# Attention and feed-forward mix: the plain input loads first on SyncE's queue, the first transposing transfers in halves

## The chip, the cores and the metric

The kernel runs on one core of one Trainium2 chip. A core has five engines, each with its own stream of instructions: TensorE (PE) multiplies matrices, VectorE (DVE) and ScalarE (ACT) work on whole tiles, GpSimd (POOL) does smaller tile work, and SyncE (SP) issues most DMA transfers. SyncE and ScalarE each have a DMA queue; in the profile SyncE's packets are counted under q1 and ScalarE's under q10. Both queues feed the same 16 DMA engines. The metric is the device time of one execution in microseconds (us).

## The reference

The inputs are x with 2,048 tokens of 512 columns in bf16, and weights. Attention has 32 heads of 16 columns, the feed-forward part an inner width of 1,792. A gate per token mixes the two:

```python
g = sigmoid((x * gate_w).sum(-1, keepdims=True))
a = attention(x, wqkv, 32 heads) @ wo       # softmax over all 2,048 tokens
b = (silu(x @ w_gate) * (x @ w_up)) @ w_down
return g * a + (1 - g) * b
```

## The kernel before

Nearly every product needs x with its columns on the partitions. That is the tile xT, `[128, 4, 2048]`: four blocks of 128 columns (dc 0 to 3), each with all 2,048 tokens. It is filled in two ways:

- By transposing DMA transfers from SyncE's queue (`queue`, line 292 on): first dc 0 and 1 for the tokens 0 to 1,023, then dc 0 to 3 for the tokens 1,024 to 2,047, one transfer of 1,024 tokens by 128 columns each, six in all.
- For dc 2 and 3 of the first 1,024 tokens by TensorE: two plain loads on ScalarE's queue (line 290) put those columns, rows as they are, into `x_rows`, a part of the tile wd_t that is needed only later. TensorE turns them, 128 by 128, by products with the identity (`turn`), and ScalarE (dc 3) and VectorE (dc 2) copy the results to xT.

Behind the row loads ScalarE's queue carries the 64 columns of K weights and the 64 columns of Q weights for the first group of heads (line 297). ScalarE spreads each into a padded tile (`pad(1)` for K, `pad(0)` for Q; the tile is called mt in the profile), and after `pad(1)` issues the load of the first 64 columns of V weights (tile rb, line 361). SyncE's queue carries, behind the transposes, the other V weights (rb), then the other K and Q weights (wqk), then the small gate column.

The opening is written out by hand. TensorE runs 12 products on zeros (`keep_warm(12)`, which write the same bank), then the 16 turns in four groups of four: dc 3 of tokens 0 to 511, dc 2 of the same, dc 3 of tokens 512 to 1,023, dc 2 of those. ScalarE's order is: the queue's issues, the table load, one small activation, `pad(1)`, the V load's issue, the copies of turn groups one and three, `pad(0)`. Then TensorE makes K for the first 1,024 tokens with eight products, and Q for the first 512 with eight half-width ones:

```python
arrived = (3, 0, 2, 1)
for tb, dc in ((tb, dc) for tb in range(2) for dc in arrived):
    mm(kp0[:, tb * QBW:(tb + 1) * QBW], lhsT=wpad[1][:, dc, :], rhs=xT[:, dc, tb * QBW:(tb + 1) * QBW],
       start=(dc == arrived[0]), stop=(dc == arrived[-1]))
```

A bound of the scores is taken from K's largest values and Q, and the first scores go to ScalarE as exponentials (tile e_all). From there a planner in the kernel's text orders the work: it keeps a model of each engine's time, and at each step writes out score products, products with V, projections or feed-forward pieces. All of that is fixed when the kernel is built; on the chip each engine runs its list in order and waits on semaphores. K of tokens 1,024 to 2,047 (`k0_pieces`) is the first side work, right behind the first scores, and needs the last four transposing transfers.

Every DMA of SyncE's and ScalarE's queues takes the next of eight semaphores in turn; a transfer waits, before it is issued, until the earlier transfer on its semaphore has landed.

Of the kernel before, what the change touches and what calls it, by code (L numbers as in the profile page):

```python
# [82 lines left out]
def kernel(  # L83
# [12 lines left out]
    nc = tc.nc  # L96
    P = 128
    x = A_x.flatten_outer_dims()
    S, D = x.shape
# [5 lines left out]
    DC = D // P  # L105
    FC = F // P
    KT = S // P
    QBW = 512
    QB = S // QBW
    TQ = QBW // P  # L110
# [171 lines left out]
    queue = Ordered(nc.sync)  # L282


    xT = big.tile([P, DC, S], BF16, name="xT")
    wd_t = big.tile([P, FC, D], BF16, name="wd_t")
    HALF = DC // 2
    x_rows = wd_t[:, 0:4, :].rearrange("p f d -> p (f d)").rearrange("p (i d) -> p i d", d=HALF * P)
    for t0 in range(2):
        nc.scalar.dma_start(out=x_rows[:, TQ * t0:TQ * t0 + TQ, :], in_=x[t0 * QBW:(t0 + 1) * QBW, HALF * P:D].rearrange("(i p) d -> p i d", p=P))  # L290
    for t0 in (0, 2 * QBW):
        for dc in range(DC if t0 else HALF):
            queue.dma_start_transpose(out=xT[:, dc, t0:t0 + 2 * QBW], in_=x[t0:t0 + 2 * QBW, dc * P:(dc + 1) * P])
    wqk = big.tile([P, DC, 2 * D], BF16, name="wqk")
    for c0 in (D, 0):

        nc.scalar.dma_start(out=wqk[:, :, c0:c0 + 64],
                            in_=A_wqkv[:, c0:c0 + 64].rearrange("(dc p) c -> p dc c", p=P))
# [5 lines left out]
    for c0 in (D, 0):  # L304
        queue.dma_start(out=wqk[:, :, c0 + 64:c0 + D],
                          in_=A_wqkv[:, c0 + 64:c0 + D].rearrange("(dc p) c -> p dc c", p=P))
# [373 lines left out]
    def q_pieces(qb, b):  # L680
        def landed(p):
            me = plan.chain
            later(0.6, lambda: end(p, me), key=("q", b))

        def rows(t, r):
            for hh in range(8):
                gg, j = hh // 4, hh % 4
                if (b, gg) != (0, 0):
                    queue.dma_start(out=get_q(qb, 2 * b + gg)[32 * j + r:32 * j + r + DH, j % 2, :],
                                      in_=t[DH * hh:DH * (hh + 1), :])  # L690

        def end(p, me):
            qst = work.tile([P, QBW], BF16, tag="qst", name="qst")
            vec.tensor_copy(out=qst[:, :], in_=p[:, :])
            m_free(p, plan.dve)
            rows(qst, 0)

            aq = work.tile([P, QBW], BF16, tag="aq", name="aq")

            def mag():  # L700
                vec.tensor_scalar(out=aq[:, :].bitcast(U16), in0=qst[:, :].bitcast(U16), scalar1=0x8000, scalar2=None,
                                  op0=ALU.bitwise_or)
                aside(weigh, QBW, lambda: rows(aq, DH), me)

            def weigh(cols):
                return gps.tensor_tensor(out=aq[:, cols], in0=aq[:, cols], in1=kb[:, b:b + 1].broadcast_to([P, QBW // 2]), op=ALU.mult)
            plan.chain = me
            later(0.21, mag, plan.dve, ("q", b), fast=True)
        return columns(DC, "qp", lambda dc: wqk[:, dc, P * b:P * (b + 1)],
                       lambda dc: xT[:, dc, qb * QBW:(qb + 1) * QBW], landed)  # L710

    def q0_pieces(qb):

        st = {}

        def landed(p):
            st["p"] = p
            later(0.6, mag, key=("aq", qb))
            later(0.21, clear, key=("aq", qb), fast=True)

        def mag():
            vec.tensor_copy(out=mt[:, 5, :], in_=st["p"][:, :])

        def clear():
            vec.tensor_scalar(out=mt[:, 5, :].bitcast(U16), in0=mt[:, 5, :].bitcast(U16), scalar1=0x7FFF, scalar2=None,
                              op0=ALU.bitwise_and)

        def bound():
            bound_add(st["p"], kneg0, mt[:, 5, :])
            spend("C", 1)  # L730
            later(0.6, lambda: apart(qb, st["p"], work.tile([P, QBW], BF16, tag="qst", name="qst")))
        return (columns(DC, "qp", lambda dc: wpad[0][:, dc, :], lambda dc: xT[:, dc, qb * QBW:(qb + 1) * QBW], landed),
                [(1, bound, False)])
# [1030 lines left out]
    for qb in range(1, QB):  # L1764
        d = qb * KT
        q, bd = q0_pieces(qb)
        q = pace.add(q, 0, d - 13, [known])
# [4 lines left out]
    for qb in range(QB):  # L1772
        for b in range(NB):
            d = UNIT.index((qb, max(2 * b, 1))) * KT
# [17 lines left out]
            q = pace.add(q_pieces(qb, b), rel, d - QLEAD, after)  # L1792
# [5 lines left out]
    turned = pace.add([(1, turn_odds, True, "F", None)], 40, 130, gates, 2)  # L1798
# [424 lines left out]
```

## Time and profile before

| | us |
|---|---|
| median of 3 runs | 747.63 |
| lowest and highest run | 747.39, 747.76 |
| profiled execution | 747.41 |
| its span, first to last instruction | 745.7 |
| TensorE, VectorE, ScalarE busy | 733.6, 713.0, 732.0 |
| GpSimd busy | 279.3 |
| first exponential (e_all) starts | 12.63 |

The views used below are the page of the profile (busy times, the chain of work that ended last), the same chain cut to the opening and told in order of time, the timeline of an engine (start, length, engine, line, operation, output and input, and in brackets the idle time before it and what ended it), one tile's groups (least, median and greatest duration in ns), and the packets of each DMA queue in a stretch of time. "ACTq" and "SPq" are the issuing of DMAs by ScalarE and SyncE; a DMA's landing has no row of its own, and shows in who waits for it. Line 261 is the helper that records every matrix product, 264 that of ScalarE's activations, 277 that of VectorE's, GpSimd's and SyncE's work, so groups are told apart by tile.

### The profile page before, as it was taken

The page shows a single profiled execution, that of the slowest core. Times are in us where ns is not written, and L with a number is a line of the kernel's source. Part 1 is how long each engine was busy: PE and PEld are TensorE (multiplying, and loading weights), DVE is VectorE, ACT ScalarE, POOL GpSimd, SP SyncE. Part 2 cuts the span into 40 slices and gives each one's busy share as a digit, 9 for nine tenths or more (in the row PEclk, how much of TensorE's full clock was granted, in tenths as well). Part 3 has the DMA queues.
Part 4 walks back from the last instruction along what each step waited for, and adds up shares of the span by engine and source line. Part 5 has one row for each costly group of instructions (what it writes and reads, how often), then busy time and mean ns, then how long its engine had stood idle before and what let it go on. Part 6 is the DMA issues. An engine that isn't in the chain of part 4 may idle for free.

```text
span 745.7 us, 24195 instructions
## 1 busy us (share of the span) xinstructions
PE 733.6 (98%) x10205; PEld 239.8 (32%) x10206; DVE 713.0 (96%) x1174; ACT 732.0 (98%) x829; POOL 279.3 (37%) x401
## 2 busy tenths in 40 slices
PE   8999999999999999999999999999999999999997
PEld 3333333333333333333333333333332333333332
DVE  7789999999999999999999999999999999999995
ACT  6999999999999999999999999999999999999996
POOL 7034432442533412544323444442245235443110
PEclk9999999999999999999999999999999999999999
DMA  9010211353220003131100141211000132100001
GB/s 198 9 44 16 57 31 37 67 142 65 65 49 14 9 24 93 42 73 38 37 17 14 41 103 34 66 34 46 18 25 16 48 94 61 32 17 15 16 30 37
DMA packets 91620, 34.92 MB, mean 47 GB/s; under 512 B 75696, under 2 KB 91064, under 8 KB 91512
## 3 DMA queue, kind: packets, MB, share of 16 engines
q1 hardware_dynamic: 88728, 32.53, 18.4%
q8 instruction: 80, 1.31, 0.7%
q10 hardware_dynamic: 2784, 0.85, 0.5%
q14 instruction: 28, 0.23, 0.1%
HBM read 21.55 MB, written 2.35 MB: 32 GB/s over the span
## 4 chain that ended last, share of the span: by engine, by line
ACT 55%; PE 35%; DVE 6%; DMA 1%; issue 1%; POOL 0%; ACTq 0%; SPq 0%; DVEq 0%; POOLq 0%
ACT e_all L264 53%; PE psum L261 35%; DVE c_t L277 4%; ACT th L264 2%; DMA wqk<-in_A_wqkv_dram 1%; DVE kaug L277 0%; DVE on L277 0%; DMA wu<-in_B_w_up_dram 0%; DVE mt L277 0%; DMA wg<-in_B_w_gate_dram 0%; DVE wd_t L277 0%; DVE gs L277 0%; DMA on<-osb 0%; ACT mt L264 0%; DVE osb L277 0%
## 5 line engine op out<-in xcount | busy, mean ns | idle before, releaser
L264 ACT ACTIVATE e_all<-psum 128x1024 bf16<-128x1024 f32 (+1 forms) x756 | 706.8, 1082 | 1.0 <-PE psum L261 0.8
L277 DVE TENSOR_SCALAR c_t<-psum 128x512 uint16<-128x512 f32 (+1 forms) x446 | 296.0, 684 | 9.0 <-PE psum L261 7.0
L261 PE MATMUL psum<-qx,kaug 32*128 32x512 bf16 (+1 forms) x1632 | 243.6, 385 | 3.3 <-ACT e_all L264 2.1
L277 POOL TENSOR_TENSOR c_t<-c_t,lift 128x256 int32<-128x256 int32 (+1 forms) x165 | 117.0, 717 | 169.2 <-DVE c_t L277 129.5
L261 PE MATMUL psum<-e_all,vaug 128*32 128x512 bf16 (+3 forms) x2004 | 166.3, 332 | 0.2 <-DVE vaug L277 0.2
L261 PEld LDWEIGHTS <-kaug 32*128 32x128 bf16 (+1 forms) x2048 | 74.6, 91 | 260.2 <-ACT e_all L264 173.1
L261 PE MATMUL psum<-c_t,vaug 128*32 128x512 bf16 (+3 forms) x1860 | 145.2, 334 | 0.9 <-DVE vaug L277 0.3
L261 PEld LDWEIGHTS <-vaug 128*32 128x32 bf16 x4152 | 99.2, 95 | 128.2 <-issue 87.7
L277 DVE TENSOR_SCALAR c_t<-c_t 128x2048 uint16<-128x2048 uint16 (+2 forms) x193 | 131.2, 686 | 1.2
L277 POOL TENSOR_TENSOR c_t<-c_t 128x256 bf16<-128x256 bf16 (+3 forms) x56 | 49.0, 886 | 73.7 <-DVE c_t L277 49.7
L261 PE MATMUL psum<-xT,wg 128*32 128x512 bf16 x896 | 73.6, 383 | 0.1
L261 PE MATMUL psum<-wd_t,mt 128*32 128x512 bf16 x896 | 72.4, 383 | 0.0
L261 PE MATMUL psum<-xT,wu 128*32 128x512 bf16 x896 | 71.7, 383 | 0.1
L261 PE MATMUL psum<-q,kaug 32*128 32x512 bf16 (+1 forms) x256 | 48.6, 385 | 0.1
L277 DVE TENSOR_SCALAR kaug<-psum 128x512 uint16<-128x512 f32 x68 | 45.0, 679 | 0.8 <-PE psum L261 0.7
L277 POOL TENSOR_TENSOR kaug<-c_t,lift 128x256 int32<-128x256 int32 (+1 forms) x38 | 26.3, 701 | 43.2 <-DVE c_t L277 35.2
L261 PE MATMUL psum<-xT,wqk 128*32 128x512 bf16 x512 | 41.0, 383 | 0.2 <-DVE c_t L277 0.2
L277 DVE TENSOR_TENSOR c_t<-c_t 128x2048 bf16<-128x2048 bf16 (+1 forms) x32 | 39.1, 1222 | 0.0
L277 DVE SCALAR_TENSOR_TENSOR gs<-th,psum 128x512 bf16<-128x512 bf16 x56 | 37.9, 677 | 1.2 <-ACT th L264 1.1
L277 DVE SCALAR_TENSOR_TENSOR mt<-gs,psum 128x512 bf16<-128x512 bf16 x56 | 37.9, 677 | 1.0 <-PE psum L261 0.5
L264 ACT ACTIVATE th<-psum 128x512 bf16<-128x512 f32 x56 | 37.3, 666 | 0.0
L277 POOL TENSOR_TENSOR aq<-aq,kb 128x256 bf16<-128x256 bf16 x32 | 19.5, 612 | 47.4 <-DVE c_t L277 33.2
(127 smaller groups left out, 479.9 us busy)
## 6 DMA issues: line engine op xcount, KB each, us to landing
wg<-in_B_w_gate_dram SPq DMA_DIRECT2D x56, 128.0 KB
wu<-in_B_w_up_dram SPq DMA_DIRECT2D x56, 128.0 KB
on<-osb SPq DMA_DIRECT2D x120, 16.0 KB
rb<-rr SPq DMA_DIRECT2D x15, 128.0 KB
wd_t<-in_B_w_down_dram SPq DMA_DIRECT2D x7, 256.0 KB
qx<-qst SPq DMA_DIRECT2D x96, 16.0 KB
qx<-aq SPq DMA_DIRECT2D x96, 16.0 KB
out_dram<-o_t SPq DMA_DIRECT2D x12, 128.0 KB
```

What stands on the lines that cost most here:

```text
L261: return ordered(nc.tensor.matmul(out, lhsT=lhsT, rhs=rhs, **kw), [lhsT, rhs], [out])
L264: ordered(nc.scalar.activation(out=out, in_=in_, **kw), [in_, *kw.values()], [out])
L277: return ordered(f(*a, **kw), reads, [out])
```

## The change

The two plain loads of rows move from ScalarE's queue to the head of SyncE's. ScalarE's queue then starts with the K and Q weights. The two transposing transfers of 1,024 tokens for the first 1,024 tokens become four of 512 tokens: dc 0 and 1 of tokens 0 to 511, then dc 0 and 1 of tokens 512 to 1,023. The four transfers for the later tokens keep their size and order. The lists of TensorE, VectorE and GpSimd are the same as before, but for the semaphores that they wait on; ScalarE's is the same without the two issues.

```diff
-    for t0 in range(2):
-        nc.scalar.dma_start(out=x_rows[:, TQ * t0:TQ * t0 + TQ, :], in_=x[t0 * QBW:(t0 + 1) * QBW, HALF * P:D].rearrange("(i p) d -> p i d", p=P))
-    for t0 in (0, 2 * QBW):
-        for dc in range(DC if t0 else HALF):
-            queue.dma_start_transpose(out=xT[:, dc, t0:t0 + 2 * QBW], in_=x[t0:t0 + 2 * QBW, dc * P:(dc + 1) * P])
+    def rows(q, t0):
+        q.dma_start(out=x_rows[:, TQ * t0:TQ * t0 + TQ, :], in_=x[t0 * QBW:(t0 + 1) * QBW, HALF * P:D].rearrange("(i p) d -> p i d", p=P))
+
+    def turned(dc, t0, n):
+        queue.dma_start_transpose(out=xT[:, dc, t0:t0 + n * QBW], in_=x[t0:t0 + n * QBW, dc * P:(dc + 1) * P])
+
+    rows(queue, 0)
+    rows(queue, 1)
+    for t0 in (0, QBW):
+        for dc in range(HALF):
+            turned(dc, t0, 1)
+    for dc in range(DC):
+        turned(dc, 2 * QBW, 2)
```

Here QBW is 512, TQ 4, DC 4, HALF 2 and P 128.

## The prediction

> **What bounds the kernel now.** I read the page's shares and chain first, then the chain of waits of the first 40 us, since all that the edit touches is issued there, then each queue in that stretch.
>
> ```profile
> span 745.7 us, 24195 instructions
> PE 733.6 (98%) x10205; PEld 239.8 (32%) x10206; DVE 713.0 (96%) x1174; ACT 732.0 (98%) x829; POOL 279.3 (37%) x401
> ACT 55%; PE 35%; DVE 6%; DMA 1%; issue 1%; POOL 0%; ACTq 0%; SPq 0%; DVEq 0%; POOLq 0%
> ```
>
> Three engines are 96 to 98% busy and DMA holds 1% of the chain. So the edit can save or cost time only in the opening; after that every engine keeps its written order of work, and a shift of the opening is passed on whole. The chain of the opening, in order of time (start, length, what):
>
> ```profile
> 0.80 0.43 ACTq L290
> ...
> 1.81 4.94 DMA wqk<-in_A_wqkv_dram
> ...
> 6.84 0.40 ACT mt L264
> ...
> 7.29 0.61 ACT xT L264
> ...
> 7.94 2.77 PE psum L261 x16
> ...
> 11.18 1.43 PE psum L261 x30
> ...
> 12.63 17.52 ACT e_all L264 x19
> ```
>
> To be seen: two row loads stand ahead of the K weights on ScalarE's queue, the weights are in use 4.94 us after their issue, ScalarE pads them (mt, 6.84), then copies the first turned block of x (xT, 7.29), and TensorE's first real product waits for that copy (7.94). From 12.63 ScalarE runs exponentials without a gap. ScalarE's own timeline, and what TensorE and VectorE do beside it:
>
> ```profile
> 0.80 0.99 ACTq L290 DMA_DIRECT2D wd_t<-in_A_x_dram  x2
> 1.81 1.11 ACTq L297 DMA_DIRECT2D wqk<-in_A_wqkv_dram  x2
> 2.95 1.28 ACT L264 ACT_TABLE_LOAD   x1 [2.95 <-issue]
> 4.25 0.20 ACT L264 ACTIVATE table<-mt 128x1 f32<-128x1 bf16 x1
> 6.84 0.44 ACT L264 ACTIVATE mt<-wqk 128x256 bf16<-128x256 bf16 x1 [2.39 <-DMA wqk<-in_A_wqkv_dram]
> 6.87 0.38 ACTq L361 DMA_DIRECT2D rb<-in_A_wqkv_dram  x1
> 7.29 1.09 ACT L264 ACTIVATE xT<-psum 128x512 bf16<-128x512 f32 x2
> ```
>
> ```profile
> 1.25 5.30 PE L261 MATMUL psum<-mt 128*128 128x512 bf16 x12 [1.25 <-DVE mt L327]
> 6.35 1.24 PE L261 MATMUL psum<-ident,wd_t 128*128 128x128 bf16 x16
> L261 PE MATMUL psum<-ident,wd_t x16: 219/219/314, 6.3 to 7.4; 128*128 128x128 bf16 x16
> 7.18 1.29 DVE L277 CAST xT<-psum 128x512 bf16<-128x512 f32 x2 [0.46 <-PE psum L261]
> 7.94 2.76 PE L261 MATMUL psum<-xT,mt 128*128 128x512 bf16 x16 [0.35 <-ACT xT L264]
> 14.21 0.62 PE L261 MATMUL psum<-xT,mt 128*32 128x512 bf16 x8
> ```
>
> ScalarE idles 2.39 us for the K weights. TensorE meanwhile runs its 12 warming products and only then, at 6.35, the 16 turns of x. They come in four groups of four; ScalarE copies groups one and three, VectorE two and four. VectorE starts the moment group two is out, 7.18; ScalarE takes group one, which was out before, only at 7.29, because the pad stands ahead of the copy. That lag is all that an earlier pad can win.
>
> SyncE's queue and the packets of the two queues (q1 is SyncE's, q10 ScalarE's; the columns are packets, MB, share), with the page's sizes of the row and weight loads, counted from the start to 7.2 us (both) and to 12 us (q1):
>
> ```profile
> 0.80 9.40 SPq L277 DMA_TRANSPOSE xT<-in_A_x_dram  x6
> 10.25 0.59 SPq L277 DMA_DIRECT2D rb<-in_A_wqkv_dram  x1
> L277 SPq DMA_TRANSPOSE xT<-in_A_x_dram x6: 1291/1432/2093, 0.8 to 8.9; - x6
> wd_t<-in_A_x_dram ACTq DMA_DIRECT2D x2, 256.0 KB
> wqk<-in_A_wqkv_dram ACTq DMA_DIRECT2D x2, 64.0 KB
> q1 hardware_dynamic: 2289, 0.57, 45.0%
> q10 hardware_dynamic: 2112, 0.66, 40.5%
> ...
> q1 hardware_dynamic: 6342, 1.59, 74.2%
> ```
>
> A transposing transfer of 1,024 tokens by 128 columns is 0.26 MB, and takes 1.29 to 2.09 us to issue. By bytes, the 0.57 MB that q1 had moved by 7.2 us are two transposes (0.52) and the start of the third, and the 1.59 MB by 12.0 all six (1.57), 1.8 us after the last issue ended.
>
> **The change, part by part.**
>
> Row loads to SyncE. ScalarE's queue loses two issues, 0.99 us; SyncE's gains them ahead of the transposes, so its first transpose is issued at 0.80 + 0.99 = 1.79 instead of 0.80. The rows are wanted at 6.35 and, for the second half, some 0.5 us later. In before their last packets are among the 2,112 of q10 by 7.2; first in a queue with only weights beside them they cannot be later. Cost nothing; the cover is the 12 warming products, which end near 6.4 whatever arrives. If the rows came after 6.4, each us late would cost one.
>
> K and Q weights. K's issue goes from 1.81 to 0.80. If its 4.94 us to use stays as it is, the pad can start at 5.74; if it takes nothing, at 3.4, for the table load and the table's first use (1.28 + 0.20, begun about 1.9) stand ahead. I take under 5.74, since fewer packets go before it. Both ends lie before 6.92 - 0.44 = 6.48, the last start that keeps the pad clear of the copy, so the difference between them is worth nothing.
>
> The first copy. The turns start over 1.24 - 0.22 = 1.02 us, so a group of four takes 0.26, and group one is out 0.26 before group two: 7.18 - 0.26 = 6.92. The copy moves from 7.29 to 6.92, or a little later since the earliest turns are the 314 ns ones: a gain of 0.32 to 0.37, I take **0.35 us**. What is late next is TensorE's own turns: they end at 7.59, and the first product, at 7.94 - 0.35 = 7.59, stands right behind them. Products follow each other at 0.21 us (four of them, 0.86). The third needs VectorE's first copy, 7.18 + 0.69 = 7.87, and comes at 8.0; the fifth needs ScalarE's second copy, about 8.1, and comes at 8.45. Neither bites. Q's pad then follows at about 8.1 with Q wanted at 9.3. So no other engine gives the gain back, and more than 0.4 us cannot be won, as the turns start at 6.35.
>
> Half transposes. Two issues of 1,024 tokens become four of 512: dc 0 and 1 of the first 512 tokens, then of the second. They are needed in the order of the products at 7.8, 8.2, 8.7 and 9.1 us (second, fourth, sixth and eighth, 0.35 earlier than now). Issue time in halves: 4 x 0.65 = 2.6 us, ending at 4.4; if a half costs as much as a whole, 4 x 1.29 = 5.2, ending at 6.95. By packets: rows, weights and two transposes are the same bytes as now, and were through by about 7.1. Issue to last packet was 1.8 us for the last transpose of before (10.2 to 12.0); with the same again, the dear end gives 8.8. The weights' last few tenths between packet and use do not show by themselves in a row. I take 7.0 to 7.5, nearest to the packet count; cost **0**, with the dear end at 0 to 0.4 us. VectorE, which fed on nothing of this, waits for TensorE only.
>
> Transposes of tokens 1,024 to 2,047. Their sixth issue now ends at 10.2. New: 4.4 + 4 x 1.43 = 10.1 with cheap halves, 6.95 + 5.72 = 12.7 with dear ones. Last packets: 11.9 or 14.5. The last of them is wanted by the eight products at 14.21, which move to 13.86. Cost **0**, or 14.5 + a few tenths - 13.86, about 1.1 us, for which TensorE would stand and the exponentials behind it. The big weight loads behind them (10.25 now) move alike by -0.1 or +2.5 us; the first of those is wanted at 19, and their bytes come within 6 us of the issue:
>
> ```profile
> 10.89 1.04 SPq L277 DMA_DIRECT2D wqk<-in_A_wqkv_dram  x2
> L261 PE MATMUL psum<-xT,wqk x16: 379/379/379, 19.1 to 19.7; 128*32 128x512 bf16 x16
> ```
>
> Waits. Each transfer reuses one of eight semaphores in turn, so the fourth half now waits for the K weights, the four long transposes for rows, Q weights, rows and the first half, and the big loads for the other halves. All those land two issues or more before; cost 0. If K were as late as today's 6.76, the fourth half would be issued then and land near 9.2, which costs 0.1 to 0.5 us. The first V columns' load (0.38, at 6.87) follows the pad and goes out 1.1 us earlier or more; it is wanted at 10.2. No other order changes on any engine.
>
> **Sum.** -0.35 against the profiled execution's 747.41 (span 745.7 and 1.7 around it): 747.06. The median of the runs is 747.63, 0.22 above the profiled one, so 747.63 - 0.35 = **747.3 us**, 0.05% less. About 0.2%, 1.5 us, is what can be told from no change here.
>
> **The rivals.**
>
> No gain (747.6). The pad is early but the first exponential stays at 12.63, because another edge of the opening ends last: a first half that lands 0.35 late (8.15 and not 7.8) does it. For it: the two row loads now delay the first transpose by 0.99 us. Against: by the bytes, rows, weights and a half transpose are 0.79 of the 1.23 MB that both queues had moved by 7.2 us; in proportion from the first issue at 0.80 that is 4.9 us, nearly 3 us early.
>
> Slower, transposes dear per piece (748.4). Place: the products at 14.21. If a half costs a whole's 1.29 us, the last long transpose is there at 14.5 and a few tenths, a stall of about 1.1 us: 747.63 - 0.35 + 1.1 = 748.4. A stall of 0.4 at the first products would only move part of the same loss forward. It decides from halves of about 1.0 us each on. For it: the smallest issue time is a floor of 1.29 seen at one size only. Against: plain loads of 512 pieces issue in 0.43 to 0.59 us, which speaks for a price by pieces.
>
> Slower, transposes that do not overlap (749.7). Should each transposing transfer wait out the one before, the two added ones cost a landing each. From issue end to last packet that is 1.8 us, 2 x 1.8 = 3.6 on top of 11.9, so 15.5 and a few tenths against 13.86: a stall of 2.0, up to 3.0 with a further delay at the first products; net +1.6 to +2.6, in the middle 749.7. Against it: four transfers (1.59 - 0.57 = 1.02 MB) went through in the 4.8 us from 7.2 to 12.0, 1.2 us each, less than the 1.29 that the issue of one takes. [...]
>
> Faster than forecast (746 or less). It would need an engine to do less work later; nothing in the edit does.
>
> **How the numbers follow.** Gain of 0.2 to 0.45 us, my forecast: 0.55. No gain, or up to 0.6 us lost: 0.20. Dear halves, +0.6 to +1.5: 0.10. In series or otherwise beyond 1.5 us: 0.12. Faster by over 1.5 us by a chance of the later order: 0.03. The first three lie within 0.2%, 0.85; slower 0.12, faster 0.03. The range from 746.8 (the full 0.45 and 0.4 of spread between medians) to 748.9 (dear halves, with half a microsecond to spare) leaves out under 2 in 10.
>
> **What would show it.** Right: ScalarE's pad before 6.5 with its wait for the weights shorter by 1 us or more; the first xT copy at 6.9 to 7.0; TensorE's first product at 7.6; the first exponential at 12.2 to 12.4; half transposes of 0.6 to 0.8 us issue, and the loads of the value weights at about 10.1. Wrong: a wait of TensorE's for a DMA of x at 8 to 10 us or at 14, halves of over 1 us, or an opening moved as said with an end that did not move along.

## The result and the profile after

The changed kernel takes 749.34 us (median of 15 runs, 747.79 to 751.07) against 747.55 us before (747.37 to 747.78): a ratio of 1.0023, 95% interval 1.0016 to 1.0029. It is 1.8 us slower, and its times scatter: seven of the 15 lie at 747.8 to 748.2, three at 749.3 to 749.8, five at 750.6 to 751.1, where those of before stay within 0.4 us. The profiled execution is one of the long ones, 750.9 us, with a span of 749.2, 3.5 more than before.

The chain of waits of the first 40 us of the changed kernel (start, length, what):

```profile
0.81 0.47 SPq L277
...
1.92 1.24 SPq L277
...
11.12 5.04 DMA xT<-in_A_x_dram
...
16.20 5.31 PE psum L261 x32
...
21.53 12.02 ACT e_all L264 x13
```

Before, this chain ran from the weights over ScalarE's pad to an unbroken row of exponentials from 12.63 us. Now SyncE's queue is the chain up to 11.12, and then the last transposing transfer, which has landed at 16.16. The queue, ScalarE and TensorE in the same stretch:

```profile
0.81 1.07 SPq L277 DMA_DIRECT2D wd_t<-in_A_x_dram  x2
1.92 10.50 SPq L277 DMA_TRANSPOSE xT<-in_A_x_dram  x8
L277 SPq DMA_TRANSPOSE xT<-in_A_x_dram x8: 1238/1279/1300, 1.9 to 11.1; - x8
```

```profile
4.70 0.44 ACT L264 ACTIVATE mt<-wqk 128x256 bf16<-128x256 bf16 x1 [1.25 <-DMA wqk<-in_A_wqkv_dram]
6.15 1.08 ACT L264 ACTIVATE xT<-psum 128x512 bf16<-128x512 f32 x2 [1.00 <-PE psum L261]
12.02 1.94 ACT L264 ACTIVATE e_all<-psum 128x1024 bf16<-128x1024 f32 x2 [0.17 <-PE psum L261]
14.48 1.02 ACT L264 ACTIVATE e_all<-psum 128x1024 bf16<-128x1024 f32 x1 [0.52 <-PE psum L261]
17.83 1.02 ACT L264 ACTIVATE e_all<-psum 128x1024 bf16<-128x1024 f32 x1 [2.33 <-PE psum L261]
```

```profile
1.25 4.63 PE L261 MATMUL psum<-mt 128*128 128x512 bf16 x12 [1.25 <-DVE mt L335]
5.72 1.06 PE L261 MATMUL psum<-ident,wd_t 128*128 128x128 bf16 x16
8.41 1.68 PE L261 MATMUL psum<-xT,mt 128*128 128x512 bf16 x11 [0.28 <-DMA xT<-in_A_x_dram]
13.72 0.40 PE L261 MATMUL psum<-xT,mt 128*32 128x512 bf16 x4 [0.58 <-DMA xT<-in_A_x_dram]
16.20 1.05 PE L261 MATMUL psum<-xT,mt 128*32 128x512 bf16 x8 [1.77 <-DMA xT<-in_A_x_dram]
22.06 0.42 PE L261 MATMUL psum<-e_all,vaug 128*32 128x512 bf16 x4
```

Three things are to be seen. The opening came forward as meant, and by more than meant: the pad is out of the way at 4.70, the first copy is at 6.15 (before 7.29), the first exponential at 12.02 (before 12.63). Each of the eight transposing transfers costs SyncE 1.24 to 1.30 us, the halves nearly as much as the wholes, so the last issue ends at 12.42 (before 10.20). And TensorE waits for x: 0.28 us for an early half, 0.58 us for the last block but one (dc 2 of the later tokens) and 1.77 us for the last (dc 3). The eight products whose first four want the last block start at 16.20 against 14.21 before, 1.99 us later.

That is not all of the 3.5 us. TensorE's work in stretches of 2 us (columns: length, busy us and instructions, granted clock, DMA share, GB/s), the changed kernel, and below it TensorE's timeline of the kernel before for the same work:

```profile
14.00:16.00 2.00, 0.44 (x6) 0.83 0.85 78
16.00:18.00 2.00, 1.79 (x14) 0.50 1.09 377
18.00:20.00 2.00, 2.00 (x16) 0.50 0.81 231
20.00:22.00 2.00, 2.00 (x12) 0.50 0.00 0
22.00:24.00 2.00, 2.00 (x34) 0.96 0.00 0
```

```profile
18.61 0.40 PE L261 MATMUL psum<-e_all,vaug 128*32 128x512 bf16 x4
```

Late in the wait, at about 15.3, the granted clock falls to 0.50, and it stays there for about 6.8 us (0.17 and 0.04 of the first and last stretch are missing, twice that at half clock, and three stretches whole). From the eight products to the same four products with V, 14.21 to 18.61 before and 16.20 to 22.06 now, TensorE takes 5.86 us in place of 4.40. Late x gives 1.99 and the slow clock 1.46, together 3.45 of the 3.5 us; nothing after 22 us adds to it. The slow clock set in some 0.9 us into the wait of 1.77 us, behind the one of 0.58.

### The profile page after: what moved, and what is told of

Its sections match the earlier page's. It is cut to its first block, busy times and chain, and to the rows that moved or that the text cites. A ratio compares the mean times of both kernels' runs of the same rounds, so it can differ in the third digit from the quotient of the medians.

```text
span 749.2 us, 24197 instructions
## 1 busy us (share of the span) xinstructions
PE 735.5 (98%) x10206; PEld 239.7 (32%) x10206; DVE 713.0 (95%) x1174; ACT 732.7 (98%) x829; POOL 279.3 (37%) x401
## 4 chain that ended last, share of the span: by engine, by line
ACT 54%; PE 33%; DVE 9%; issue 2%; SPq 1%; DMA 1%; POOL 0%; DVEq 0%; POOLq 0%
ACT e_all L264 51%; PE psum L261 33%; DVE c_t L277 5%; ACT th L264 2%; SPq L277 1%; DVE kaug L277 1%; DVE gs L277 1%; DVE mt L277 1%; DMA xT<-in_A_x_dram 1%; DVE on L277 0%; DMA wg<-in_B_w_gate_dram 0%; DVE wd_t L277 0%; DVE osb L277 0%; POOL c_t L277 0%; DVE vaug L277 0%
```

## The experiments

| run | what differs | median us (range) | ratio to before, 95% |
|---|---|---|---|
| e1 | the change, first two transposes whole (6) | 747.17 (747.10 to 747.24) | 0.9997, 0.9989 to 1.0006 |
| e2 | before, first two transposes halved (8) | 747.11 (746.79 to 747.42) | 0.9997, 0.9988 to 1.0005 |
| e3 | the change again | 749.73 (749.19 to 750.35) | 1.0032, 1.0020 to 1.0044 |
| e4 | before, weights ahead of the rows | 749.24 (748.55 to 751.93) | 1.0031, 1.0020 to 1.0041 |
| e5 | the change, two transposes of 2,048 tokens (4) | 749.37 (749.07 to 751.00) | 1.0026, 1.0016 to 1.0036 |
| e6 | the change, zeros in TensorE's wait | 749.92 (749.72 to 750.35) | 1.0035, 1.0022 to 1.0047 |
| e7 | the change, only dc 0 halved (7) | 746.70 (746.56 to 746.77) | 0.9991, 0.9982 to 0.9999 |
| e8 | before, halves and two of 1,536 tokens (6) | 748.58 (748.36 to 748.78) | 1.0016, 1.0008 to 1.0025 |
| e9, e10 | the change again | 750.53, 750.49 (747.78 to 751.32) | 1.0045, 1.0029 to 1.0062; 1.0034, 1.0022 to 1.0046 |

In brackets behind the words is the number of transposing transfers. The medians of before beside them were 747.35 to 747.41.

**e1, the change without the halving.**

```diff
-    for t0 in (0, QBW):
-        for dc in range(HALF):
-            turned(dc, t0, 1)
+    for dc in range(HALF):
+        turned(dc, 0, 2)
```

> The change without the halving: the rows first on SyncE, the weights alone on ScalarE, and the first two transposing transfers whole, so six issues in place of eight. Theory A (a transposing transfer costs SyncE 1.24 to 1.30 us to issue, whether of 512 or of 1,024 tokens): the last issue ends at 1.9 + 6 x 1.3 = 9.7 us, TensorE does not wait for x at 13 to 17 us, its granted clock stays 1.0 from 14 to 22 us, and the kernel is 0.3 to 0.7 us faster than before (746.9 to 747.3), since ScalarE's pad is out of the way of the first copy. Rival B (the rows ahead of the transposes on SyncE's queue are what makes them late): TensorE still waits for x, 747.8 to 751.

747.17 us, and steady. Of SyncE's queue and TensorE:

```profile
1.87 8.94 SPq L277 DMA_TRANSPOSE xT<-in_A_x_dram  x6
8.37 2.11 PE L261 MATMUL psum<-xT,mt 128*128 128x512 bf16 x13 [0.68 <-DMA xT<-in_A_x_dram]
14.00 0.61 PE L261 MATMUL psum<-xT,mt 128*32 128x512 bf16 x8
```

The last issue ends at 10.81, later than the 9.7 expected because one issue took 2.25 us, and the eight products do not wait. Rival B is out: rows on SyncE and weights alone on ScalarE cost nothing by themselves. The gain is smaller than theory A had it, because the second whole transpose is now late for the first products, by 0.68 us; that was the halves' use.

**e2, the halving alone.** In the kernel before:

```diff
-    for t0 in (0, 2 * QBW):
-        for dc in range(DC if t0 else HALF):
-            queue.dma_start_transpose(out=xT[:, dc, t0:t0 + 2 * QBW], ...)
+    for t0 in (0, QBW):
+        for dc in range(HALF):
+            turned(dc, t0, 1)
+    for dc in range(DC):
+        turned(dc, 2 * QBW, 2)
```

> Only the halving, on the kernel before: rows and weights on ScalarE's queue as they were. Theory A: eight issues of 1.3 us or more from 0.8, so the last ends at 11.2 us or later (before: six from 0.8 to 10.2, three of them stretched); TensorE waits for x at 13 to 17 us, and the time is 747.8 to 750, spread over more than 1 us. Rival B: no wait beyond those of before, 747.4 to 747.8.

My expectation was wrong: 747.11 us, not slower at all.

```profile
0.80 10.54 SPq L277 DMA_TRANSPOSE xT<-in_A_x_dram  x8
L277 SPq DMA_TRANSPOSE xT<-in_A_x_dram x8: 1235/1280/1315, 0.8 to 10.0; - x8
13.74 0.61 PE L261 MATMUL psum<-xT,mt 128*32 128x512 bf16 x8
```

The price of an issue is as theory A says, 1.24 to 1.32 us for halves and wholes alike. But eight of them from 0.80 end at 11.34, and the products at 13.74 are still served in time. So neither half of the change is harmful alone: e1 puts 1.02 us of row loads ahead of six transposes, e2 puts two more issues in, and only both together, 12.42, pass the point from which TensorE waits.

**e7, one halving in place of two.**

```diff
-    for t0 in (0, QBW):
-        for dc in range(HALF):
-            turned(dc, t0, 1)
+    turned(0, 0, 1)
+    turned(1, 0, 2)
+    turned(0, QBW, 1)
```

> The change with only dc 0 halved: seven transposing transfers. Price theory: last issue ends at 1.9 + 7 x 1.3 = 11.0 us plus what stretches, between 10.8 (whole, no wait at 13 us) and 12.4 (the change). If 11.4 as in the halving alone is still in time, TensorE does not wait at 13 to 17 us and the time is 747.0 to 747.6; if it ends later than about 11.7, a wait of under 1 us and 747.5 to 749. Rival (the count does not matter, only weights alone on ScalarE's queue together with any half): 749 or more.

746.70 us, below the 747.0 to 747.6 expected, the fastest of all and 0.66 us under the kernel before beside it, with an interval that just excludes 1 (up to 0.9999).

```profile
1.87 9.23 SPq L277 DMA_TRANSPOSE xT<-in_A_x_dram  x7
11.88 4.69 ACT L264 ACTIVATE e_all<-psum 128x1024 bf16<-128x1024 f32 x5 [0.16 <-PE psum L261]
13.46 0.62 PE L261 MATMUL psum<-xT,mt 128*32 128x512 bf16 x8
```

Seven issues end at 11.10; TensorE waits for no transfer of x, early or late, and the exponentials run unbroken from 11.88, 0.75 earlier than before, where the span is 0.8 shorter (744.9). Against the change this takes away one issue of 1.3 us, by joining the halves of dc 1, and nothing else. Its eight products start at 13.46, earlier than in the change, so an early opening that wants x sooner is not what makes the change wait. By the number of transposes the last issue ends at 10.81, 11.10, 11.34 without a wait (e1, e7, e2), and at 12.42 with one.

**e3, e9 and e10, the change again, for more profiled executions.**

> The changed kernel once more, for a second profiled execution. Theory A with the clock: the time goes by whether TensorE's granted clock drops to 0.5 after the wait for x. If the execution profiled here is a short one (748.2 or less), the clock stays at 1.0 from 14 to 22 us and the wait for the last transpose is under 1.2 us; if it is a long one (750.5 or more), 6 to 7 us at 0.5 as in the first profile. Rival C (the length of the wait alone makes the spread): a short execution shows a wait shorter by the whole difference, some 2.5 us, and the long ones no more than their wait.

> The changed kernel again, in search of a profiled execution among its short times. If it is short (748.2 or less): last issue of a transpose still at 12.4 us, but TensorE's wait for x under 1.2 us and the granted clock at 1.0 from 14 to 22 us. If long (749 or more): a wait of 1.7 us or more, the clock at 0.5 for 3.4 us or 6.8 us behind it, and an instruction fetch of 16 KB on the DMA engines that overlaps the last transposes.

> As the run before it: short with a wait under 1.2 us and the clock at 1.0, or long with a wait of 1.7 us or more and a stretch at 0.5.

e3's profiled execution was a long one (750.35 us), e9's and e10's short ones (747.85 and 747.78). TensorE where the last blocks come, e3 first, then e9, with e9's first exponential below:

```profile
15.20 0.62 PE L261 MATMUL psum<-xT,mt 128*32 128x512 bf16 x4 [2.38 <-DMA xT<-in_A_x_dram]
...
16.00:18.00 2.00, 2.00 (x16) 0.50 1.09 379
```

```profile
9.40 1.25 PE L261 MATMUL psum<-xT,mt 128*128 128x512 bf16 x9 [0.39 <-DMA xT<-in_A_x_dram]
14.70 0.62 PE L261 MATMUL psum<-xT,mt 128*32 128x512 bf16 x8 [0.40 <-DMA xT<-in_A_x_dram]
16.00:18.00 2.00, 1.81 (x19) 1.00 1.06 363
12.58 2.86 ACT L264 ACTIVATE e_all<-psum 128x1024 bf16<-128x1024 f32 x3 [0.17 <-PE psum L261]
```

In both the last issue ends at 12.4. In the short one TensorE waits 0.40 us, keeps its clock, and the eight products are 0.49 later than before (14.70 and 14.21); the span, 746.1, is 0.4 longer. Nor has the opening gained: TensorE waits 0.29 and 0.39 us for early halves, and the first exponential is at 12.58 (12.48 in e10), where it was 12.63 before. That is the price of the late issues alone.

The two long ones with a profile have a wait of 1.8 to 2.4 us and the slow clock on top, in e3 for 3.4 us (0.20 and 0.15 of the stretches around 16 to 18 are missing), half of what the first profile had. Rival C, which put the whole scatter on the wait, falls for these two: waits of 0.3 to 0.4 and of 1.77 to 2.38 us differ by 1.4 to 2.1, the spans 746.1 and 748.6 to 749.2 by 2.5 to 3.1, and the rest falls in the time at half clock.

It does not fall for all. Of the 32 executions of the changed kernel on record ten lie at 747.8 to 748.2, six at 749.2 to 749.8 and 16 at 750.1 to 751.3. By estimate, a stretch like that of e3, 3.4 us at half clock, takes 0.0023 off the mean granted clock of an execution (0.5 times 3.4 of some 749 us). The 14 executions above 750.3 have a mean of 0.995 to 0.997; the three lowest of the middle group, 749.19, 749.20 and 749.34, have 0.999, which leaves no room for such a stretch. As far as the mean clock can tell, these are slow by the late x alone, by 1.2 to 1.5 us more than the short ones; none of them was profiled.

In e3 it is not the last issue that TensorE waits for. Its 2.38 us are for the last block but one, whose issue ran from 9.73 to 11.02 and which landed at 15.15. In e7 and e2 issues that ended at 11.10 and 11.34 were in time for products at 13.46 and 13.74. With the 2.3 us from the end of issue to landing that e9 had, e3's block would by estimate have been there at 13.3. So the late issue is the price that the short executions pay, and the two long ones profiled pay for a transfer that stalls once it is issued. By the packets' own times, the last packet of x was through 1.7 and 1.8 us after the end of the last issue in e9 and e10, and 2.9 and 3.1 us after it in the first profile and in e3.

Why the same transfer lands at 14.7 or at 16.2 is seen in part. In all of these a 16 KB fetch of instructions (queue q8) goes over the DMA engines about then. The packets of e3 from 12 to 14 us and from 14.3 to 15.1, then those of e9 from 12 to 14:

```profile
q1 hardware_dynamic: 1197, 0.30, 179.3%
q8 instruction: 1, 0.02, 4.2%
...
q1 hardware_dynamic: 35, 0.01, 9.1%
```

```profile
q1 hardware_dynamic: 1607, 0.42, 109.0%
q8 instruction: 1, 0.02, 2.9%
```

In e3 the fetch starts at 12.99, while the last two transposes are under way, and from 14.3 to 15.1 SyncE's queue moves 35 packets; in e9 it starts at 13.97, and all but two of x's 6,144 packets are through by 14. The first profile is closer to e9 than to e3: its fetch starts at 13.87, with 34 packets of x still to end after 14, and the last of them ends at 15.35. In e10 the fetch starts at 13.91, 11 packets end after 14, and the last is through at 14.15, without a stall. In the kernel before and in e1, e2 and e7 the last packet of x is through over 1 us before the fetch. So a stall is seen only where the fetch came before x was through, but not each time, and nothing here moved the fetch by itself: that it is the cause is an inference and not shown.

**e6, TensorE kept busy through the wait.** Ten products by zeros (40 instructions) ahead of the one that waits for the last block, into the same sum. Of the edit, the lines that add them (`fill` is 10 for this one sum and 0 elsewhere):

```diff
+                for i in range(4 * fill if k == n - 1 else 0):
+                    j = i % 4
+                    mm(st["p"][32 * j:32 * j + 32, :], lhsT=idle[:, 0:32], rhs=rhs(0), start=False, stop=False,
+                       tile_position=(0, 32 * j), skip_group_check=True)
```

> The changed kernel with ten products by zeros (40 instructions, 2.2 us at full clock) put ahead of the one that waits for the last transpose, adding nothing to its sum. Transfers and waits stay as they are. Clock theory: TensorE no longer idles over 1 us there, the granted clock stays 1.0 from 14 to 22 us, no product takes over 0.45 us after 14 us, and the time is 747.6 to 748.8 in every run, 1 us or more under the changed kernel. Rival (the late x alone is the loss): 749 to 751 as without the zeros, or worse by what they take.

```profile
14.28 2.77 PE L261 MATMUL psum<-xT,mt 128*32 128x512 bf16 x48
16.00:18.00 2.00, 2.00 (x32) 1.00 1.02 336
PE psum L261 <- DMA qx<-qst: 0.7, 1, 0.7
```

The clock stayed at 1.00 in every stretch from 6 to 24 us, as expected. The gain did not come: 749.92 us, within the rival's 749 to 751. Here the zeros took their 2.2 us (2.77 for the 48 instructions, against 0.62 for the eight alone in e9), and a wait of 0.7 us for another transfer (qx) came on top, at 35.7. But this execution is no test of a long wait: its first exponential was late (12.69), as in the short executions of the changed kernel, whose clock stayed at 1.00 without any zeros, and x was there before the zeros ended. So e6 shows neither that work through a long wait keeps the clock nor a saving. It shows only that its five executions lie within 0.7 us of each other, with mean clocks of 0.998 to 0.999. What the slow clock costs rests on the like stretches above, 1.46 us in the first profile.

**e4, weights ahead of the rows on ScalarE's queue,** the transposes as before:

```diff
+    for c0 in (D, 0):
+        nc.scalar.dma_start(out=wqk[:, :, c0:c0 + 64], ...)
     for t0 in range(2):
         nc.scalar.dma_start(out=x_rows[:, TQ * t0:TQ * t0 + TQ, :], ...)
-    wqk = big.tile(...)
-    for c0 in (D, 0):
-        nc.scalar.dma_start(out=wqk[:, :, c0:c0 + 64], ...)
```

> Only the order on ScalarE's queue changed in the kernel before: K and Q weights, then the rows; SyncE's queue as before, with six transposes. The pad's wait for the weights ends by 5.7 us, the rows are there by 6.4, the first copy moves from 7.29 to 6.9 to 7.0, the first exponential from 12.63 to 12.3. Theory: 0.3 to 0.4 us faster than before (747.2). Rival: the turns of x wait for rows that are now later, and nothing is won (747.5 to 748).

```profile
6.70 0.62 PE L261 MATMUL psum<-ident,wd_t 128*128 128x128 bf16 x8 [0.34 <-DMA wd_t<-in_A_x_dram]
8.99 0.66 PE L261 MATMUL psum<-ident,wd_t 128*128 128x128 bf16 x8 [1.66 <-DMA wd_t<-in_A_x_dram]
10.00:12.00 2.00, 2.00 (x7) 0.50 1.10 237
```

The rival won, by more than it said (749.24 us where it had 747.5 to 748): the second half of the rows comes 1.66 us after TensorE wants it, and the clock drops here too. The pad was early (4.35), and it was of no use. What lets the weights go first in the change is that the rows lead SyncE's queue.

**e5 and e8, longer transposes.** e5 is the change with `turned(dc, 0, 4)` for dc 0 and 1 and `turned(dc, 2 * QBW, 2)` for dc 2 and 3; e8 is e2 with `turned(dc, t0, n)` for (t0, n) of (0, 1) and (QBW, 3), then dc 2 and 3 of the later tokens.

> Price of one transposing transfer by its length: dc 0 and 1 each in one transfer of 2,048 tokens, then dc 2 and 3 of the later 1,024, rows first on SyncE: four issues. If the price is one per transfer whatever its length, the long ones issue in about 1.3 us and the last issue ends near 7.1 us; if 1.3 us is a floor and length counts above it, the long ones take 2.5 us or more and the last issue ends at 9.5 to 10. In both cases the second block of x comes later than the first K products want it (two long transfers are 1.05 MB, by about 9.5 to 10 us), so that TensorE waits for x at 7 to 10 us by 1 to 2 us, and the time is 747.5 to 750, the more if the clock drops.

> A try for a better order: rows and weights on ScalarE's queue as before; transposes of dc 0 and 1 for the first 512 tokens, then of dc 0 and 1 for the other 1,536 in one transfer each, then dc 2 and 3 of the later 1,024: six issues with the first halves early. If issue goes by transfers, the last ends near 8.7 us; if by length over a floor, near 9.5. Gain: first exponential at 12.1 to 12.3, 746.9 to 747.3. Loss, if the first 1,536-token transfers come later than about 8.5 and 9 us, when the second half of the K products wants them: 747.5 to 748.5.

```profile
L277 SPq DMA_TRANSPOSE xT<-in_A_x_dram x4: 1297/1840/3497, 1.9 to 9.2; - x4
10.46 3.79 PE L261 MATMUL psum<-xT,mt 128*128 128x512 bf16 x13 [1.21 <-DMA xT<-in_A_x_dram]
```

```profile
L277 SPq DMA_TRANSPOSE xT<-in_A_x_dram x6: 1243/1298/2166, 0.8 to 8.9; - x6
10.61 1.25 PE L261 MATMUL psum<-xT,mt 128*128 128x512 bf16 x9 [1.27 <-DMA xT<-in_A_x_dram]
```

The shortest issues took 1.24 us for 512 tokens (e8) and 1.28 to 1.30 for 1,024 (1.28 in e1 and e4, 1.30 in e5). Longer ones: issues of 1,536 tokens took 1.95 and 2.17 us and issues of 2,048 took 2.32 and 3.50; but single issues of 1,024 tokens took 2.25 us in e1 and 2.62 in e4 too, so how much of this is length is not shown. The four issues of e5 end at 10.48 and the six of e8 at 10.23, no earlier than the six of before (10.20), and the block of dc 1 that the early products want is 1.2 to 1.3 us late. Both are slower, e5 at 749.37 within its 747.5 to 750, e8 at 748.58 just past its 747.5 to 748.5.

## Why the prediction was wrong

The price of a half is the step that failed. "Issue time in halves: 4 x 0.65 = 2.6 us" was measured at 4 x 1.25, that is 5.0. With it fell the cost of 0 for the later transposes: their last issue ended at 12.42 and not at 10.1, and TensorE waited for them, 0.3 to 0.4 us in the short executions profiled and 1.8 to 2.4 us in the long ones. I had a floor of 1.29 us in view at one size, gave the dear end as a bound, and chose the cheap one by the likeness to plain loads of 512 pieces, which issue in 0.5 us. The transposing transfers here were not like them: 512 and 1,024 tokens cost nearly the same, 1.24 to 1.26 and 1.30 us in the changed kernel. The dear end of the next step, last issue at 12.7, was close (12.42), partly by luck: the four long transposes were priced at 1.43 us and came 1.34 apart. The place of the loss, the eight products behind the first scores, was that of the rival "transposes dear per piece". That rival's chance of 0.10 was too low.

Its size was too small as well. It had 1.1 us of stall and no more. The short executions lose less, 0.5 at that place, and end at 747.8 to 748.2, within the range. The profiled long ones wait 1.8 to 2.4 us and then run at half clock, in the first profile 1.46 us more. A second term failed there: "Issue to last packet was 1.8 us", carried over from before, held in the short ones (1.7 and 1.8) and not in the long ones (2.9 and 3.1). Neither the clock nor the scatter was in any case of mine, and the median, 749.34, fell past the upper end of 748.9. That execution had a mean granted clock of 0.999, so what took it there is the late x and hardly the clock. Seven of the 15 executions were short, so where the median of the mixture falls is partly chance.

The first copy: right in kind, too small in size. "More than 0.4 us cannot be won, as the turns start at 6.35" took the warming products for fixed. They took 5.30 us in the profile of before and 4.11 to 5.30 in the others, so the turns came at 5.20 to 6.35 where the rows were there in time. What varies is the moment from which they follow each other at 0.21 us and no longer at 0.43: in the profile of before none did, in e9 those from 4.1 us on. With the pad out of the way, the opening came forward by up to 0.9 us (e3's first exponential at 11.70 against 12.63) and, in the changed kernel, x was wanted that much earlier than I had reckoned.

The weights: right, in use at 4.70 where 3.4 to 5.74 was given. The rows: right, no turn waits for them; and as e4 shows, the condition that they lead a queue mattered. The wait of each transfer for the earlier one on its semaphore: right at a cost of 0, as the transposes' issues stand 0.04 us apart in the changed kernel. That a shift of the opening is passed on whole: right, 3.45 us at 22 us and 3.5 at the end, and in e7 0.75 and 0.8.

"Transposes that do not overlap" gave 749.7, near the measured time, for a reason that did not occur: issues followed each other at 1.3 us and stood 0.04 us apart, so no landing was waited for.

What stays open: why x lands 1.5 us later in the long executions at the same issue times, what the fetch of instructions has to do with it, and why the shares of short and long executions are what they are.

## What to carry to other kernels

Price each transfer by the issuing queue, per kind and per size, before cutting it: here a half transpose issued hardly faster than a whole one (1.24 to 1.26 us against 1.30), so a cut buys an earlier first part at the full price of an issue for all that stands behind. Two edits that are each harmless may use up one margin together; find the margin (here the last issue could move from 10.20 to 11.34 without a wait, and not to 12.42) and try the edit with one step less, as e7 did. A wait on TensorE near the margin cost more than its own length here where the clock dropped with it (1.46 us on top of 1.99 in the first profile), and showed as scatter between executions.

## What was not expected of the hardware

- A transposing transfer took its queue at the least 1.23 us for 512 tokens by 128 columns (e7) and 1.28 us for 1,024 (e1 and e4), against 0.5 us for a plain load of 256 KB (0.47 and 0.54 in the changed kernel); single issues of 1,024 tokens took up to 2.62 us (e4).
- Waits of TensorE far shorter than the stretch that followed came with a granted clock of 0.50: 0.58 and 1.77 us (first profile, 6.8 us at 0.50), 2.38 us (e3, 3.4 us), 0.34 and 1.66 us (e4) and 0.60 and 1.21 us (e5). One of 1.27 us (e8) did not, nor one of 0.40 us (e9), so the length of a wait alone does not decide it.
- The 12 warming products of the same kernel took 4.11 us in one execution (e9) and 4.64 in another (e10): they follow each other at 0.43 us at first and at 0.21 us later, from 4.1 us on in e9 and from 5.1 in e10.
